# Batch 0 with more filler matmuls and a later exp, loads queued two batches ahead, attention moved within the experts' matmuls

## The chip, the cores and the metric

The kernel runs on one core of one Trainium2 chip. The metric is the device time of one execution in microseconds (us). Three runs of the kernel before gave 232.02, 232.46 and 232.63 us, median 232.46. The profile and the trace are of one further execution, which took 234.29 us. Engines are named as in the profile: PE (matrix multiplications; PEld is its weight load), ACT (activations), DVE (elementwise work), POOL (here it issues the loads), SP (here it issues the stores).

## What is computed

For each of 8 batches: linear attention over 8 heads (sequence 576, head size 64) with a normalisation, then one expert of 8 for the whole batch, chosen by a router on the mean over the sequence.

```python
kv  = einsum('bhsd,bhse->bhde', k, v)
out = einsum('bhsd,bhde->bhse', q, kv)
out = out / sqrt(mean(out * out, -1) + 1e-6) * g_norm
x   = out.transpose(0, 2, 1, 3).reshape(B, S, H * D)     # 8 x 576 x 512
logits = x.mean(1) @ w_gate                              # 8 experts
e_idx  = argmax(logits, 1)
y[b]   = softmax(logits)[b, e_idx] * (relu(x[b] @ w1[e_idx]) @ w2[e_idx])   # 512 -> 1024 -> 512
```

## The kernel before, in words

Everything is written for one batch at a time, and the order of the work on each engine is the order in which the program issues it. A load is converted from 32 to 16 bits on its way in.

The attention of a batch works on four pairs of heads, c = 0 to 3. Its pieces are small functions:

- `s_kv` (L115): 48 matmuls make k^T v of all pairs (12 for one pair), DVE casts them into the block matrices `kvb` (L128, L129). Called kv(b) here.
- `s_qt` (L102), called T(c): 12 transposes of q on PE, copied by DVE (L113).
- `s_o` (L131), called O(c): two matmuls (L135), then on ACT the square (L138), and on DVE a copy of the result (L143; batch 0 has none and reads PSUM later).
- `s_m` (L146), called M(c): two matmuls with `ones` take the mean of the squares (L151), then ACT does ln (L154) and exp (L155), which give one over the root.
- `s_x` (L158), called X(c): DVE multiplies and writes xT (L163), with the sum over the sequence as a by-product.
- `s_gate` (L167), `s_gate2` (L175), `s_gate3` (L203): the router. `s_gate2` has one small matmul (L178), finds the largest logit on DVE, POOL reads the index, and issues the loads of that expert's weights w1 (L194) and w2 (L196), called w(b), and behind them loads of q, k and v of a later batch (L64).

The expert of a batch (called MoE b) is cut into 18 units: 8 units `m_1` (L207; 8 matmuls L215 and a relu on ACT, L218) and 10 units `m_2` (L220; tiles t = 0 to 3 with 4 matmuls L244 a unit, and the smaller t = 4, L231). After two tiles DVE scales the result (L248, and L237 for t = 4) and SP stores it.

The program first runs the attention of batch 0 by itself, with filler matmuls (`warm`, L97; 128x512, into a tile that is written over) in between, then eight steps of batch 1. From there on it goes through the 8 x 18 units in order; after each unit it issues what the list `after` holds for that unit. `att_steps` (L284) cuts the attention of a batch into 17 steps, 0 to 16, for successive units: kv; T(0); T(1); O(0) and T(2); O(1); T(3) and M(0); O(2) and X(0); M(1); O(3) and X(1); M(2); M(3) and X(2); X(3) and gate; none; none; gate2; none; gate3. The line with `at` (L303) says behind which unit step 0 stands: unit 13 for batch 2, and unit 18(b-2)+3 for the others, so the attention of b runs within MoE b-2.

All loads that matter go through one queue, which POOL fills and which works in order. Four sets of q, k and v fit in SBUF, three sets of weights, and each PSUM tag ("a" for attention, "m" for the expert) has two buffers.

Of the kernel before, what the change touches and what calls it, by code (L numbers as in the profile page):

```python
# [17 lines left out]
def kernel(  # L18
# [36 lines left out]
    st = [dict() for _ in range(B)]  # L55

    def load_qkv(b, parts, which=None):
        if kvq[b] is None:
            kvq[b] = [pqkv.tile([P, H, NJ, Dh], F16, tag=n, name=n) for n in ("kt", "vt", "qt")]
        step = H // parts  # L60
        for i in (range(parts) if which is None else which):
            for t, src in zip(kvq[b], (k, v, q)):
                hs = slice(i * step, (i + 1) * step)
                nc.gpsimd.dma_start(  # L64
                    t[0:R, hs], src[b, hs].rearrange("h (p j) d -> p h (j d)", j=NJ))
# [25 lines left out]
    def psum(tag):  # L91
        return ps.tile([P, 2, 512], F32, tag=tag, name="ps_" + tag)

    def two(t):
        return t.rearrange("p (i n) -> p i n", i=2)

    def warm(t, n):  # L97
        for _ in range(n):
            nc.tensor.matmul(t[:, 1, :], ones, kvb[:, 1], start=True, stop=True)  # L99


    def s_qt(b, c, w=0):  # L102
        s = st[b]
        if "qT" not in s:
            s["qT"] = att.tile([P, NP, S], F16, tag="qT", name="qT")
        p32 = psum("a")
        warm(p32, w)
        pt = p32.bitcast(F16)
        for j in range(NJ):
            for i in range(2):  # L110
                nc.tensor.transpose(pt[64 * i:64 * i + 64, 0, j * R:(j + 1) * R],  # L111
                                    kvq[b][2][0:R, 2 * c + i, j, :], ident[0:R, 0:R])
        nc.vector.tensor_copy(s["qT"][:, c, :], pt[:, 0, 0:S])  # L113

    def s_kv(b, prs, w=0):  # L115
        kt, vt = kvq[b][0:2]
        kv = kvb[:, b % 2]
        p32 = psum("a")
        warm(p32, w)
        pk = p32[:, 0].rearrange("p (c e) -> p c e", c=NP)  # L120
        for c in prs:
            for j in range(NJ):
                for i in range(2):
                    nc.tensor.matmul(pk[64 * i:64 * i + 64, c, 64 * i:64 * i + 64],  # L124
                                     kt[0:R, 2 * c + i, j, :], vt[0:R, 2 * c + i, j, :],
                                     start=(j == 0), stop=(j == NJ - 1))
        cs = slice(prs[0], prs[-1] + 1)
        nc.vector.tensor_copy(kv[0:64, cs, 0:64], pk[0:64, cs, 0:64])  # L128
        nc.vector.tensor_copy(kv[64:128, cs, 64:128], pk[64:128, cs, 64:128])  # L129

    def s_o(b, c, tag="a"):  # L131
        s = st[b]
        po = psum(tag)
        for i in range(2):
            nc.tensor.matmul(po[:, i, 0:HS], kvb[:, b % 2, c, :],  # L135
                             s["qT"][:, c, i * HS:(i + 1) * HS], start=True, stop=True)
        sq = sm.tile([P, S], F16, tag="sq", name="sq")
        nc.scalar.activation(two(sq), po[:, :, 0:HS], AF.Square)  # L138
        if b == 0:
            o = po[:, :, 0:HS]  # L140
        else:
            o = two(sm.tile([P, S], F32, tag="o", name="o"))
            nc.vector.tensor_copy(o, po[:, :, 0:HS])  # L143
        s["sq", c], s["o", c] = sq, o

    def s_m(b, c):  # L146
        s = st[b]
        sq = s["sq", c]
        pm = psum("a")
        for i in range(2):  # L150
            nc.tensor.matmul(pm[:, i, 0:HS], ones, sq[:, i * HS:(i + 1) * HS],  # L151
                             start=True, stop=True)
        ln = sm.tile([P, S], F32, tag="ln", name="ln")
        nc.scalar.activation(two(ln), pm[:, :, 0:HS], AF.Ln, bias=epsc)  # L154
        nc.scalar.activation(ln, ln, AF.Exp, scale=-0.5)  # L155
        s["ln", c] = ln

    def s_x(b, c):  # L158
        s = st[b]
        if "xT" not in s:  # L160
            s["xT"] = xp.tile([P, NP, S], F16, tag="xT", name="xT")
            s["pl"] = sm.tile([P, NP], F32, tag="pl", name="pl")
        nc.vector.scalar_tensor_tensor(out=two(s["xT"][:, c, :]), in0=s["o", c], scalar=gcol,  # L163
                                       in1=two(s["ln", c]), op0=ALU.mult, op1=ALU.mult,
                                       accum_out=s["pl"][:, c:c + 1])
# [9 lines left out]
    def s_gate2(b):  # L175
        s = st[b]
        pg = psum("a")[:, 0, 0:E]
        nc.tensor.matmul(pg, mean, s["ts"], start=True, stop=True)  # L178
        mx = sm.tile([P, 8], F32, tag="mx", name="mx")
        ix = sm.tile([P, 8], U32, tag="ix", name="ix")  # L180
        nc.vector.max(mx, pg)
        nc.vector.max_index(ix, mx, pg)
        nm = sm.tile([P, 1], F32, tag="nm", name="nm")
        nc.vector.tensor_scalar(out=nm, in0=mx[:, 0:1], scalar1=-1.0, scalar2=None, op0=ALU.mult)
        lg = sm.tile([P, E], F32, tag="lg", name="lg")
        gs = sm.tile([P, 1], F32, tag="gs", name="gs")
        nc.scalar.activation(lg, pg, AF.Exp, bias=nm, accum_out=gs)
        ev = nc.gpsimd.value_load(ix[0:1, 0:1], min_val=0, max_val=E - 1)
        w1 = wp.tile([P, 4, F], F16, tag="w1", name="w1")
        w2 = wp.tile([P, 8, D], F16, tag="w2", name="w2")  # L190
        nh = 2 if b in (0, B - 1) else 1
        for h in range(nh):
            fs = slice(h * F // nh, (h + 1) * F // nh)
            nc.gpsimd.dma_start(w1[:, :, fs],  # L194
                                moe_w1[ds(ev, 1), :, fs].rearrange("o (c p) f -> p (o c) f", p=P))
        nc.gpsimd.dma_start(w2, moe_w2[ds(ev, 1)].rearrange("o (c p) d -> p (o c) d", p=P))  # L196
        s["w"] = (w1, w2)
        s["gs"] = gs
        for n in {0: (2,), 1: (3, 4)}.get(b, (b + 3,)):
            if n < B:  # L200
                load_qkv(n, 1)

# [62 lines left out]

    warm(psum("a"), 8)
    for c in range(NP):
        s_kv(0, [c], 1)  # L270
        s_qt(0, c, 1)
        if c > 0:
            s_m(0, c - 1)
        s_o(0, c, "m")
        if c > 0:
            s_x(0, c - 1)
    s_m(0, 3)
    warm(psum("a"), 9)
    s_x(0, 3)
    s_gate(0)  # L280
    s_gate2(0)


    def att_steps(b, early=False):  # L284
        T, M, X = (lambda c, f=f: (lambda: f(b, c)) for f in (s_qt, s_m, s_x))
        O = lambda c: (lambda: s_o(b, c, "m" if early and c < 3 else "a"))
        return [[lambda: s_kv(b, [0, 1, 2, 3], 4 if early else 0)],
                [T(0)], [T(1)], [O(0), T(2)], [O(1)], [T(3), M(0)], [O(2), X(0)], [M(1)],
                [O(3), X(1)], [M(2)], [M(3), X(2)], [X(3), lambda: s_gate(b)], [], [],
                [lambda: s_gate2(b)], [], [lambda: s_gate3(b)]]  # L290
# [7 lines left out]
    NU = 18  # L298
# [1 line left out]
    for i, e in enumerate(a1[n1:]):  # L300
        after[i] += e
    for b in range(2, B):
        at = 13 if b == 2 else NU * (b - 2) + 3  # L303
        for i, e in enumerate(att_steps(b)):
            after[at + i] += e
    for b in range(B):
# [34 lines left out]
```

## Time and profile before

| | |
|---|---|
| median of three runs | 232.46 us |
| the profiled execution, its own time | 234.29 us |
| its span in the trace | 232.6 us |
| PE busy | 193.7 us (83%) |
| ACT busy | 107.9 us (46%) |
| DVE busy | 98.0 us (42%) |
| POOL busy | 39.9 us (17%) |
| moved by DMA | 40.67 MB, mean 175 GB/s |

In the trace, the first unit of MoE 0 starts at 34.2 us, that of MoE 1 at 56.8, MoE 2 at 98.3, MoE 3 at 124.2, MoE 4 at 147.6, MoE 5 at 170.9, MoE 6 at 194.2 and MoE 7 at 210.5. A batch with attention in it takes 23.3 us from there on, one without 16.3 us.

How to read the lines: a row of waits gives the waiting engine with its line, who ended the wait, the sum in us, how often, and the longest. A row in order of time gives the start, the duration, the engine, the line, output<-input, shape and count; in square brackets stands how long the engine was idle before it and what released it. A row of stages gives, for a stretch of the span, the busy us and instructions of PE, PEld, DVE, ACT and POOL, then the clock granted to PE (1.00 is full), the busy share of the DMA engines and GB/s. A row of DMA issues ends with the KB and the us from issue to landing. The clock reads 1.00 until the first change that the record holds, so for the first stretch the durations have to tell it.

### The profile page before, as it was taken

How to read it: one execution, taken by the hardware profiler on the slowest of the kernel's cores; microseconds unless marked ns; L12 is line 12 of the kernel's file. 1: busy time of each engine (PE TensorE's matmuls, PEld its weight loads, DVE VectorE, ACT ScalarE, POOL GpSimd, SP SyncE). 2: the span in 40 equal slices, each digit the busy share in tenths (PEclk: the TensorE clock that was granted, in tenths of full speed). 3: DMA queues.
4: the chain of work that ended last, by engine and by line, in shares of the span. 5: the costliest groups of instructions: out<-in, count | busy, mean ns of one | idle time of the engine just before them, and what ended most of it. 6: DMA issues, size and time to landing. Idle time of an engine off the chain costs nothing.

```text
span 232.6 us, 4436 instructions
## 1 busy us (share of the span) xinstructions
PE 193.7 (83%) x1837; PEld 118.6 (51%) x1837; DVE 98.0 (42%) x232; ACT 107.9 (46%) x177; POOL 39.9 (17%) x58
## 2 busy tenths in 40 slices
PE   6896859997707989299898989898989898999990
PEld 1443436654505655167556755675567556747640
DVE  1243564246321449403394339533953385022040
ACT  2166079502903568034683468346834683504400
POOL 7920250280000006321002300200020002100000
PEclk9999999999965699859999999999999999999997
DMA  5999099999999905999999999999969933996033
GB/s 50 180 195 188 1 175 198 204 210 249 245 204 203 163 0 73 208 256 204 208 209 247 246 209 208 246 248 211 212 191 183 189 82 102 183 210 199 1 90 113
DMA packets 39141, 40.67 MB, mean 175 GB/s; under 512 B 2242, under 2 KB 31954, under 8 KB 39122
## 3 DMA queue, kind: packets, MB, share of 16 engines
q0 software_dynamic: 32592, 30.95, 83.4%
q1 hardware_dynamic: 6530, 9.44, 13.1%
q8 instruction: 14, 0.23, 0.4%
q14 instruction: 5, 0.04, 0.0%
HBM read 61.88 MB, written 9.44 MB: 307 GB/s over the span
## 4 chain that ended last, share of the span: by engine, by line
PE 46%; DMA 21%; ACT 12%; DVE 11%; issue 5%; POOL 1%; POOLq 1%; DVEq 0%
PE ps_m L215 25%; DMA vt<-in_v_dram 12%; PE ps_m L244 9%; DMA w<-in_moe_w_dram 7%; DVE ot L248 4%; ACT ln L154 4%; DVE o L143 3%; ACT sq L138 3%; PE ps_a L151 3%; PE ps_a L124 3%; DMA out_dram<-ot 3%; ACT hT L218 2%; PE ps_a L111 2%; PE ps_a L99 2%; DVE xT L163 2%
## 5 line engine op out<-in xcount | busy, mean ns | idle before, releaser
L215 PE MATMUL ps_m<-xT,w 128*128 128x288 f16 x512 | 73.9, 299 | 11.4 <-DMA w<-in_moe_w_dram 6.5
L218 ACT ACTIVATE hT<-ps_m 128x576 f16<-128x576 f32 x64 | 41.5, 650 | 52.9 <-PE ps_m L215 52.7
L215 PEld LDWEIGHTS <-w 128*128 128x128 f16 x512 | 50.5, 103 | 27.8 <-DMA w<-in_moe_w_dram 7.2
L244 PE MATMUL ps_m<-w,hT 128*128 128x512 f16 x256 | 61.8, 379 | 0.0
L244 PEld LDWEIGHTS <-hT 128*128 128x128 f16 x256 | 24.8, 98 | 22.8
L194 POOL DMA_DIRECT2D w<-in_moe_w_dram x10 | 7.6, 759 | 148.6 <-PE ps_m L215 58.6
L248 DVE TENSOR_SCALAR ot<-ps_m,gates 128x1024 f32<-128x1024 f32 x16 | 20.5, 1284 | 29.5 <-PE ps_m L244 27.3
L154 ACT ACTIVATE ln<-ps_a,epsc 128x576 f32<-128x576 f32 x32 | 23.6, 738 | 15.3 <-PE ps_a L151 15.2
L143 DVE COPY o<-ps_a 128x576 f32<-128x576 f32 x25 | 18.9, 756 | 27.5 <-ACT sq L138 27.5
L163 DVE SCALAR_TENSOR_TENSOR xT<-o,gcol,ln 128x576 f16<-128x576 f32 x28 | 22.4, 814 | 3.9 <-ACT ln L155 3.9
L155 ACT ACTIVATE ln<-ln 128x576 f32<-128x576 f32 x32 | 21.9, 683 | 1.0
L138 ACT ACTIVATE sq<-ps_a 128x576 f16<-128x576 f32 x25 | 16.0, 641 | 10.8 <-PE ps_a L135 10.2
L113 DVE COPY qT<-ps_a 128x576 f16<-128x576 f16 x32 | 14.5, 453 | 14.7 <-PE ps_a L111 14.6
L128 DVE CAST kvb<-ps_a 64x256 f16<-64x256 f32 (+1 forms) x11 | 3.8, 343 | 35.8 <-PE ps_a L124 35.8
L151 PE MATMUL ps_a<-sq,ones 128*128 128x288 f16 x64 | 14.6, 313 | 5.0 <-ACT sq L138 1.6
L111 PE MATMUL ps_a<-ident,qt 96*64 96x96 f16 x384 | 15.7, 223 | 2.2 <-ACT ln L154 0.9
L111 PEld LDWEIGHTS <-qt 96*64 96x64 f16 x384 | 11.3, 119 | 11.9 <-issue 9.3
L124 PE MATMUL ps_a<-vt,kt 96*64 96x64 f16 x384 | 9.3, 208 | 8.3 <-DMA vt<-in_v_dram 8.3
L99 PE MATMUL ps_a<-kvb,ones 128*128 128x512 f16 x29 | 13.2, 582 | 2.0 <-DVE ones L85 2.0
L124 PEld LDWEIGHTS <-kt 96*64 96x64 f16 x384 | 8.1, 123 | 13.1 <-issue 12.2
L151 PEld LDWEIGHTS <-ones 128*128 128x128 f16 x64 | 6.1, 102 | 11.2 <-issue 5.3
L135 PE MATMUL ps_a<-qT,kvb 128*128 128x288 f16 x50 | 10.2, 285 | 1.9 <-DVE o L143 1.8
(41 smaller groups left out, 103.1 us busy)
## 6 DMA issues: line engine op xcount, KB each, us to landing
w<-in_moe_w_dram POOLq DMA_DIRECT2D x14, 1024.0 KB, 16.3
out_dram<-ot SPq DMA_DIRECT2D x24, 192.0 KB, 5.1
kt<-in_k_dram POOLq DMA_DIRECT2D x7, 576.0 KB, 20.4
vt<-in_v_dram POOLq DMA_DIRECT2D x7, 576.0 KB, 22.5
qt<-in_q_dram POOLq DMA_DIRECT2D x7, 576.0 KB, 24.6
out_dram<-ot SPq DMA_DIRECT2D x40, 64.0 KB, 4.8
w<-in_moe_w_dram POOLq DMA_DIRECT2D x4, 512.0 KB, 7.2
out_dram<-ot SPq DMA_DIRECT2D x16, 128.0 KB, 5.1
```

Source lines behind the costliest of these rows:

```text
L111: nc.tensor.transpose(pt[64 * i:64 * i + 64, 0, j * R:(j + 1) * R], kvq[b][2][0:R, 2 * c + i, j, :], ident[0:R, 0:R])
L124: nc.tensor.matmul(pk[64 * i:64 * i + 64, c, 64 * i:64 * i + 64], kt[0:R, 2 * c + i, j, :], vt[0:R, 2 * c + i, j, :], start=(j == 0), stop ...
L138: nc.scalar.activation(two(sq), po[:, :, 0:HS], AF.Square)
L143: nc.vector.tensor_copy(o, po[:, :, 0:HS])
L151: nc.tensor.matmul(pm[:, i, 0:HS], ones, sq[:, i * HS:(i + 1) * HS], start=True, stop=True)
L154: nc.scalar.activation(two(ln), pm[:, :, 0:HS], AF.Ln, bias=epsc)
L155: nc.scalar.activation(ln, ln, AF.Exp, scale=-0.5)
L163: nc.vector.scalar_tensor_tensor(out=two(s["xT"][:, c, :]), in0=s["o", c], scalar=gcol, in1=two(s["ln", c]), op0=ALU.mult, op1=ALU.mult, a ...
L215: nc.tensor.matmul(ph[:, i, 0:HS], w1[:, c, fb * P:(fb + 1) * P], s["xT"][:, c, i * HS:(i + 1) * HS], start=(c == 0), stop=(c == 3))
L218: nc.scalar.activation(two(s["hT"][:, fb, :]), ph[:, :, 0:HS], AF.Relu)
L244: nc.tensor.matmul(po[:, t % 2, :], s["hT"][:, fc, t * P:(t + 1) * P], w2[:, fc, :], start=(fc == 0), stop=(fc == 7))
L248: nc.vector.tensor_scalar(out=ot, in0=po, scalar1=gates[:, b:b + 1], scalar2=None, op0=ALU.mult)
```

## The change

It has four edits. Batch 0 gets more fillers: 10 instead of 8 ahead of it, 2 instead of 1 in each call of `s_kv` and `s_qt`, and 3 ahead of the last M. In batch 0 the exp of a pair is issued behind the square of the next pair. The loads of q, k and v of batch b+2 are queued behind w(b) for all b; before, it was batch 2 behind w(0), batches 3 and 4 behind w(1) and b+3 behind w(b). And for batches 3 to 7, step 0 of the attention stands behind unit 18(b-2)+2b-2, which is 4, 6, 8, 10 and 12 units into MoE b-2 instead of 3 for all.

```diff
-    def s_m(b, c):
+    def s_m(b, c, exp=True):
...
         nc.scalar.activation(two(ln), pm[:, :, 0:HS], AF.Ln, bias=epsc)
+        s["ln", c] = ln
+        if exp:
+            s_e(b, c)
+
+    def s_e(b, c):
+        ln = st[b]["ln", c]
         nc.scalar.activation(ln, ln, AF.Exp, scale=-0.5)
-        s["ln", c] = ln
...
-        for n in {0: (2,), 1: (3, 4)}.get(b, (b + 3,)):
+        for n in (b + 2,):
             if n < B:
                 load_qkv(n, 1)
...
-    warm(psum("a"), 8)
+    warm(psum("a"), 10)
     for c in range(NP):
-        s_kv(0, [c], 1)
-        s_qt(0, c, 1)
+        s_kv(0, [c], 2)
+        s_qt(0, c, 2)
         if c > 0:
-            s_m(0, c - 1)
+            s_m(0, c - 1, False)
         s_o(0, c, "m")
         if c > 0:
+            s_e(0, c - 1)
             s_x(0, c - 1)
+    warm(psum("a"), 3)
     s_m(0, 3)
     warm(psum("a"), 9)
...
-        at = 13 if b == 2 else NU * (b - 2) + 3
+        at = 13 if b == 2 else NU * (b - 2) + 2 * b - 2
```

Three places show how rows move. The first is ACT's queue in batch 0, from the second row on (sq, ln: L138, L154; exp is L155 before and L161 after). Before:

```order
L138 ACTIVATE sq_170<-ps_m_167 128x576
L154 ACTIVATE ln_206<-ps_a_203,epsc_109 128x576
L155 ACTIVATE ln_206<-ln_206 128x576
L138 ACTIVATE sq_212<-ps_m_209 128x576
L154 ACTIVATE ln_251<-ps_a_248,epsc_109 128x576
L155 ACTIVATE ln_251<-ln_251 128x576
```

After:

```order
L138 ACTIVATE sq_174<-ps_m_171 128x576
L154 ACTIVATE ln_212<-ps_a_209,epsc_109 128x576
L138 ACTIVATE sq_217<-ps_m_214 128x576
L161 ACTIVATE ln_212<-ln_212 128x576
L154 ACTIVATE ln_259<-ps_a_256,epsc_109 128x576
L138 ACTIVATE sq_264<-ps_m_261 128x576
L161 ACTIVATE ln_259<-ln_259 128x576
```

The square of the next pair now stands between a pair's ln and its exp.

The second is POOL's queue from the weights of batch 1 to those of batch 2 (kt, vt, qt are k, v and q of one batch; w1 and w2 an expert's weights; ix the index that the router found). Before:

```order
L196 DMA w2_622<-in_moe_w2_dram 128x8x512
L64 DMA kt_625<-in_k_dram 96x8x384
L64 DMA vt_626<-in_v_dram 96x8x384
L64 DMA qt_627<-in_q_dram 96x8x384
L64 DMA kt_631<-in_k_dram 96x8x384
L64 DMA vt_632<-in_v_dram 96x8x384
L64 DMA qt_633<-in_q_dram 96x8x384
L188 TENSOR_LOAD ix_1106
L188 ISA x2
L194 ISA
L194 DMA w1_1123<-in_moe_w1_dram 128x4x1024
```

After:

```order
L201 DMA w2_636<-in_moe_w2_dram 128x8x512
L64 DMA kt_639<-in_k_dram 96x8x384
L64 DMA vt_640<-in_v_dram 96x8x384
L64 DMA qt_641<-in_q_dram 96x8x384
L193 TENSOR_LOAD ix_1094
L193 ISA x2
L199 ISA
L199 DMA w1_1111<-in_moe_w1_dram 128x4x1024
L201 ISA
L201 DMA w2_1112<-in_moe_w2_dram 128x8x512
L64 DMA kt_1115<-in_k_dram 96x8x384
L64 DMA vt_1116<-in_v_dram 96x8x384
```

Batch 3 (kt_625, now kt_639) keeps its place. Batch 4 (kt_631, now kt_1115) moves from ahead of batch 2's router and weights to behind them.

The third is DVE in the second half of MoE 2, where the attention of batch 4 runs (o is the copy L143, xT is X, ot the scaled output: L248 before, L253 after). Before:

```order
L113 COPY qT_1367<-ps_a_1459 128x576
L143 COPY o_1488<-ps_a_1483 128x576
L163 SCALAR_TENSOR_TENSOR xT_1490,pl_1491<-o_1421,gcol_85,ln_1476 128x576
L248 TENSOR_SCALAR ot_1507<-ps_m_1454,gates_119 128x1024
L143 COPY o_1518<-ps_a_1513 128x576
```

After:

```order
L143 COPY o_1473<-ps_a_1468 128x576
L253 TENSOR_SCALAR ot_1479<-ps_m_1420,gates_119 128x1024
L113 COPY qT_1405<-ps_a_1485 128x576
L143 COPY o_1515<-ps_a_1510 128x576
L168 SCALAR_TENSOR_TENSOR xT_1517,pl_1518<-o_1448,gcol_85,ln_1502 128x576
L143 COPY o_1539<-ps_a_1534 128x576
L168 SCALAR_TENSOR_TENSOR xT_1517,pl_1518<-o_1473,gcol_85,ln_1527 128x576
L253 TENSOR_SCALAR ot_1546<-ps_m_1505,gates_119 128x1024
L168 SCALAR_TENSOR_TENSOR xT_1517,pl_1518<-o_1515,gcol_85,ln_1555 128x576
```

The first scaling of an output now stands ahead of T(3) and of the first X, and the second one ahead of the last two X; before, all four X stood ahead of the second scaling. On PE, kv(3) moves behind one more unit of MoE 1 (unit 4, with M(2) of batch 2), and kv(4) from behind the fourth to behind the seventh unit of MoE 2.

## The prediction

> **What bounds the kernel now.** I read the page's busy shares and slices first, then PE's waits, then the time order around the longest waits.
>
> ```profile
> PE 193.7 (83%) x1837; PEld 118.6 (51%) x1837; DVE 98.0 (42%) x232; ACT 107.9 (46%) x177; POOL 39.9 (17%) x58
> PE   6896859997707989299898989898989898999990
> PEclk9999999999965699859999999999999999999997
> PE ps_a L124 <- DMA vt<-in_v_dram: 8.3, 2, 7.7
> PE ps_m L215 <- DMA w<-in_moe_w_dram: 6.5, 3, 4.2
> PE ps_m L215 <- DVE ot L248: 4.0, 5, 0.9
> ```
>
> PE is busy for 83% and no other engine reaches half, so PE's order and what PE waits for set the time. The PE row dips at the start, in slices 11 and 12 and in slice 16. The three rows of waits say what the dips are: one wait of 7.7 us for v, waits of up to 4.2 us for weights, and many small ones for an output tile. The clock row drops at the same two places.
>
> ```profile
> 70.16 1.49 PE L124 MATMUL ps_a<-vt,kt 96*64 96x64 f16 x48 [7.70 <-DMA vt<-in_v_dram]
> 79.50:80.00 0.50, 0.50 (x5) 0.36 (x4) 0.16 (x1) 0.31 (x1) 0.00 (x0) 0.77 1.21 207
> 85.51 0.28 PE L178 MATMUL ps_a<-ts,mean 128*128 128x8 f32 x2
> 88.58 9.69 DMA w<-in_moe_w_dram
> 98.32 6.67 PE L215 MATMUL ps_m<-xT,w 128*128 128x288 f16 x32 [4.18 <-DMA w<-in_moe_w_dram]
> 104.92 0.95 PE L124 MATMUL ps_a<-vt,kt 96*64 96x64 f16 x48
> 124.23 4.08 PE L215 MATMUL ps_m<-xT,w 128*128 128x288 f16 x32 [0.90 <-DVE ot L248]
> ```
>
> These rows are a chain. kv(3) starts at 70.16 when v of batch 3 lands; the router matmul of batch 2 follows at 85.51; its weights are issued at 88.58, and the first half takes 9.69 us; MoE 2 starts at 98.32; kv(4) at 104.92. The clock (the third figure from the end of a windows row) is back up at 79.7, where it averages 0.77. From 105 on PE hardly waits. A load that is issued late moves all that follows.
>
> **Prologue: a gain of 1.3 us, taken.** Batch 0 runs a ring over three engines.
>
> ```profile
> 2.04 4.02 PE L99 MATMUL ps_a<-kvb,ones 128*128 128x512 f16 x9 [2.04 <-DVE ones L85]
> 12.20 0.74 ACT L154 ACTIVATE ln<-ps_a,epsc 128x576 f32<-128x576 f32 x1 [1.99 <-PE ps_a L151]
> 13.57 0.63 ACT L138 ACTIVATE sq<-ps_m 128x576 f16<-128x576 f32 x1
> 15.04 0.64 PE L151 MATMUL ps_a<-sq,ones 128*128 128x288 f16 x2 [0.22 <-DVE kvb L129]
> 19.22 0.74 ACT L154 ACTIVATE ln<-ps_a,epsc 128x576 f32<-128x576 f32 x1 [1.51 <-PE ps_a L151]
> 21.94 0.74 ACT L154 ACTIVATE ln<-ps_a,epsc 128x576 f32<-128x576 f32 x1 [0.73 <-PE ps_a L151]
> 25.33 0.28 PE L178 MATMUL ps_a<-ts,mean 128*128 128x8 f32 x2
> 25.55 1.02 PE L99 MATMUL ps_a<-kvb,ones 128*128 128x512 f16 x4
> 84.40 0.41 PE L151 MATMUL ps_a<-sq,ones 128*128 128x288 f16 x2 [0.29 <-DVE o L143]
> ```
>
> The ring goes from one ln to the next in 3.51 us (two turns from 12.20 to 19.22): ln, exp, xT on DVE, the casts of the next kv, the mean matmul M. A filler takes 4.02/9 = 0.45 us here and 0.25 us at 25.55, so PE is at half speed up to there. The new start is 12 fillers, kv and 2 fillers without a gap, about 5.5 us. At 98.32 the rise took some 5.3 us of unbroken matmuls, so I expect full speed from about 7.5. Then transposes (0.69 to 0.45 for twelve, by the rows at 75.05 and 83.67 below), M (0.64 to 0.41) and kv with the fillers around it are quicker ahead of the first ln, which comes about 0.9 earlier. Against it: with exp behind the next square, the square's 0.63 is inside the ring, while M shrinks from 0.64 to 0.41. A turn costs 0.4 more, and there are two: 0.8 lost. At the end the last ln no longer waits behind that exp: 21.94 less 19.22 is 2.72, and becomes 2.1; 0.6 gained. The router matmul now ends the queue of nine fillers (25.33, when its input was ready at 24.7); at full speed those are over first: another 0.6. Sum -0.9 + 0.8 - 0.6 - 0.6 = -1.3. Bounds: -2.1 (no turn grows) and +2.3 (half speed throughout, below). The gain reaches the end, since w(0) and every load behind it queue on this router.
>
> A rule weighs against this step. The Trainium skill, page "TensorE: Matmul & The Clock Gate", section "Part 4: PE-mode transpose", says that transposes do not count as PE activity for the clock. By it the prologue, a fifth of it transposes, could stay at half speed and the term would be the +2.3 bound. The trace agrees only in part: at 83.67, with the clock up, twelve transposes take 0.45 us, against 0.69 at 75.05 with the clock down, so a raised clock holds through them; whether they help to raise it no row shows.
>
> **From kv(3) to w(2): -3.3 us.** vt(3) has the same loads ahead of it as before, so kv(3) keeps its 70.16 less the prologue. It now sits one unit later; PE does m_1 unit 4 and M(2) in the wait, which falls from 7.7 to about 6.1.
>
> ```profile
> 71.58 2.10 PE L215 MATMUL ps_m<-xT,w 128*128 128x288 f16 x8
> 73.47 0.69 PE L151 MATMUL ps_a<-sq,ones 128*128 128x288 f16 x2
> 75.05 0.69 PE L111 MATMUL ps_a<-ident,qt 96*64 96x96 f16 x12 [0.89 <-ACT ln L154]
> 83.67 0.45 PE L111 MATMUL ps_a<-ident,qt 96*64 96x96 f16 x12
> 84.65 1.02 PE L244 MATMUL ps_m<-w,hT 128*128 128x512 f16 x4
> ```
>
> Between kv(3) and the router of batch 2 (85.51 - 70.16 = 15.35) three pieces go: the unit, 1.89 (71.58 to 73.47), M(2) with the wait behind it, 1.58 (to 75.05), and T(3) with M(0), 0.98 (83.67 to 84.65), which come after the router now. That is 4.45, of which I give back 1.45, because about that much of what stays falls into the 9.5 us at half clock. Net -3.0, bounds -4.4 and -2. From router to issue took 3.07 (85.51 to 88.58), and 2.30 for batch 0 (25.33 to 27.63); I take -0.3 between 0 and -0.8.
>
> **A new wait at kv(4): +7.8 us.** This is the largest term.
>
> ```profile
> vt<-in_v_dram POOLq DMA_DIRECT2D x1, 576.0 KB, 22.3
> 90.99 0.78 POOL L64 DMA_DIRECT2D vt<-in_v_dram  x1
> 27.63 1.51 POOL L194 DMA_DIRECT2D w<-in_moe_w_dram  x2 [14.61 <-issue]
> 82.00:94.00 12.00, 11.08 (x79) 5.95 (x77) 8.79 (x23) 8.28 (x14) 3.95 (x5) 1.00 0.34 50
> ```
>
> Before, k/v/q of batch 4 went out before w(2), and the queue had run dry by 82, so kv(4) waited for nothing. Now they stand behind w(2), in the place of batch 5, whose v landed at 90.99 + 22.3 = 113.3, 24.7 us after w(2)'s issue. The 22.3 row is the larger of two; k comes 2.1 earlier. Nothing ahead of it in the queue is different, so I carry 24.7 over, give or take 1. Before, kv(4) came 104.92 - 88.58 = 16.3 after that issue; it is now 8.4 later. But three more m_1 units are done ahead of it (4.08/4 = 1.0 each, 3.2 with the change between forms): -3.2. As a check: w1(2) at 9.7, four units at half speed 6.6, the router 0.3, three units 3.2, so PE is there at 19.8 and waits 4.9. The DMA slots of 82 to 94 (share 0.34) lie idle even longer, which is the cause. A wait of 4.2 put the clock down at 98.32 and cost 6.67 - 4.08 = 2.6 over four units; the same again here: +2.6, between 0 (a wait under about 3) and 4.8 (half of the 9.5 us after 70.16). Sum 8.4 - 3.2 + 2.6 = +7.8. Later loads have 26 units of lead against 15 for batch 4, and PE is then the slower.
>
> **Attention placed 6 to 12 units into each MoE, instead of 3: +0.5 us.**
>
> ```profile
> 122.94 0.39 PE L178 MATMUL ps_a<-ts,mean 128*128 128x8 f32 x2 [0.26 <-DVE ts L172]
> 135.27 0.41 PE L135 MATMUL ps_a<-qT,kvb 128*128 128x288 f16 x2 [0.36 <-DVE o L143]
> 137.20 0.41 PE L151 MATMUL ps_a<-sq,ones 128*128 128x288 f16 x2 [0.29 <-DVE o L143]
> L248 DVE TENSOR_SCALAR ot<-ps_m,gates 128x1024 f32<-128x1024 f32 x16 | 20.5, 1284 | 29.5 <-PE ps_m L244 27.3
> 39.22 1.14 PE L215 MATMUL ps_m<-xT,w 128*128 128x288 f16 x8 [0.17 <-ACT hT L218]
> 41.10 2.12 PE L215 MATMUL ps_m<-xT,w 128*128 128x288 f16 x16 [0.74 <-ACT hT L218]
> ```
>
> A batch with attention has four waits now: 0.90 (124.23), 0.26, 0.36, 0.29, 1.81 in all, so 7.24 for batches 4 to 7. The first two go where X(3) falls behind the output copies; the other two stay, and the output copies of 1.28 in DVE's queue between square and copy of o lengthen them for batches 5 to 7: my count is 0.8, 1.05, 1.5, 1.5, sum 4.85. Nine m_1 units lose their 0.09 for a change of form: -0.8. Against it, ln and exp of late batches meet the relu of the next MoE. MoE 0 shows that with the steps of batch 1 (as batch 6 now): 0.17 + 0.74 = 0.9. Batch 7 has two more M there (each a ln of 0.74 and an exp of about that on ACT): 2.2; batch 5 one: 0.4. Sum 4.85 + 3.5 - 7.24 - 0.8 = +0.3, taken as +0.5, bounds -6.5 (no wait left but the relu's) and +4.
>
> **w(7): +0.7 us.**
>
> ```profile
> w<-in_moe_w_dram POOLq DMA_DIRECT2D x1, 512.0 KB, 5.6
> 202.02 7.07 PE L244 MATMUL ps_m<-w,hT 128*128 128x512 f16 x32
> 210.47 8.00 PE L215 MATMUL ps_m<-xT,w 128*128 128x288 f16 x64 [0.38 <-DVE ot L248]
> ```
>
> The router of batch 7 moves to unit 8 of MoE 6. Router to issue 2.1 to 2.3, first part 5.6: 7.8. From there PE has 7 units of 0.88, the last tile 1.06 and the 0.38: 7.6. I add 0.5 for output stores in the same engines; bounds 0 and 3.
>
> **Sum.** -1.3 - 3.3 + 7.8 + 0.5 + 0.7 = **+4.4 us**. The profiled execution took 234.29 us (span 232.6) and would become 238.7; it is 1.8 above the median of the runs, 232.46, and I predict against the median: **236.9 us**, slower by 1.9%.
>
> **Rivals.** (1) *Faster: the placement pays.* If ACT's bursts vanish behind the two ps_m buffers and no DVE wait grows, that term is -6.5 and the total -2.6: 229.9. It decides once four batches shorten by over 1.15 us each. For it: the 0.90 waits clearly come from DVE order. Against: 39.22 and 41.10 show relu waits reaching PE. Chance 0.12. (2) *No change: kv(4) waits under 3 us*, because w(2) goes out or lands 2 us sooner; then the clock stays up too: -2 - 2.6, total -0.2, 232.3. Against: 24.7 is a measured landing. Chance 0.10. (3) *The fillers do not raise the clock.* Sixteen more, at 0.43 each, of which the last groups hide: the router of batch 0 comes at 27.6 instead of 25.33: +2.3 for -1.3, 240.5. For it: nine fillers in a row, 4.02 us, did not raise it. Chance 0.14. The forecast has 0.64.
>
> Below 0.3% (0.7 us) a measurement of this kernel cannot tell a change from none. Faster 0.12, same 0.10, slower 0.78. The range leaves out rival 1 and about as little above rival 3: 232.2 to 241.2; without the rivals it would be 234.4 to 239.4.
>
> **What would show it.** Right: fillers of 0.22 us from about 7.5 on; ln to ln 3.9; batch 0's router near 24.0; a wait for v of about 6 us and a second, new one of 4 to 6 ending some 15 us after MoE 2's start, with the clock at 0.5 after it; relu waits at the start of MoE 6. Wrong: no second wait for v, or MoE 3 to 6 under 22.5 us each.

## The result and the profile after

Four runs of the changed kernel took 242.62 to 245.79 us, median 244.08; the kernel before, on the same chip, 232.55. The ratio is **1.050, interval 1.043 to 1.0575**: slower by 11.5 us, and above the range. Ratios and intervals here leave out the executions that were over 1.5% slower than the quickest of their kernel; the medians keep them, so a ratio is not always that of the medians. The profiled execution took 242.62 us (span 241.0), the quickest of its four, while the one of before was 1.8 us above its median; the two profiles therefore differ by 8.3 us only. The sums below are made between the profiles.

The page of the changed kernel: busy time, slices of PE, its clock and the DMA rate.

```profile
PE 191.5 (79%) x1850; PEld 116.6 (48%) x1850; DVE 98.2 (41%) x232; ACT 105.9 (44%) x177; POOL 39.9 (17%) x58
PE   6877778999259879149989988998889798986690
PEclk9999979999959999758999999999999999999798
GB/s 60 189 195 149 63 200 203 206 228 255 210 125 4 33 165 279 211 207 209 205 240 192 194 204 226 178 195 209 241 181 135 210 207 0 69 201 253 25 86 110
```

The rows of PE's waits in it (who was waited for, sum, times, longest):

```profile
PE ps_a L124 <- DMA vt<-in_v_dram: 15.5, 2, 8.5
PE ps_m L220 <- ACT hT L223: 4.2, 8, 0.8
PE ps_m L249 <- DMA w<-in_moe_w_dram: 3.8, 1, 3.8
PE ps_m L220 <- DMA w<-in_moe_w_dram: 3.6, 4, 1.5
```

PE fell from 83% to 79%. The wait for v now comes twice, 15.5 us against 8.3. Relu (hT) holds up the next unit eight times, 4.2 us in all (before twice, 0.9 us), and one group is new: L249, the second half of an expert, waits 3.8 us for weights. The slices, counted from one, show where: 17 and 18 (the second wait for v) and 37 and 38 (the last MoE), each with the clock down in it or beside it. The DMA engines stand nearly still in slices 13 and 14, as they did before in 15 and 16 (0 and 73 GB/s). (The prediction counts the slices from zero.)

The time order of PE in the changed kernel (start, duration, the wait in brackets); L220 and L249 are L215 and L244 of before.

```profile
68.97 1.49 PE L124 MATMUL ps_a<-vt,kt 96*64 96x64 f16 x48 [7.03 <-DMA vt<-in_v_dram]
78.79 0.28 PE L183 MATMUL ps_a<-ts,mean 128*128 128x8 f32 x2
105.51 1.49 PE L124 MATMUL ps_a<-vt,kt 96*64 96x64 f16 x48 [8.51 <-DMA vt<-in_v_dram]
123.33 1.91 PE L220 MATMUL ps_m<-xT,w 128*128 128x288 f16 x13 [0.96 <-DVE ot L253]
212.54 4.09 PE L220 MATMUL ps_m<-xT,w 128*128 128x288 f16 x32 [0.65 <-DMA w<-in_moe_w_dram]
217.17 4.09 PE L220 MATMUL ps_m<-xT,w 128*128 128x288 f16 x32 [0.53 <-DMA w<-in_moe_w_dram]
225.04 8.77 PE L249 MATMUL ps_m<-w,hT 128*128 128x512 f16 x32 [3.77 <-DMA w<-in_moe_w_dram]
```

Issues of weights from POOL's time order: first w(7) in the kernel before (its w(2), at 88.58, is among the prediction's rows), then w(2) and w(7) in the changed kernel:

```profile
196.28 1.49 POOL L194 DMA_DIRECT2D w<-in_moe_w_dram  x2 [21.68 <-DVE gates L204]
```

```profile
81.20 0.77 POOL L199 DMA_DIRECT2D w<-in_moe_w_dram  x1 [32.99 <-DVE qT L113]
206.61 1.49 POOL L199 DMA_DIRECT2D w<-in_moe_w_dram  x2 [24.54 <-DVE gates L209]
```

Before, w(7) went out 14.2 us ahead of the start of MoE 7 (210.47), now 5.9 us (212.54).

The start of the last scaling on DVE closes the account, first of before and then of the changed kernel:

```profile
226.62 0.47 DVE L237 TENSOR_SCALAR ot<-ps_m,gates 128x256 f32<-128x256 f32 x1
```

```profile
235.04 0.48 DVE L242 TENSOR_SCALAR ot<-ps_m,gates 128x256 f32<-128x256 f32 x1
```

| stretch | before, us | after, us | difference | the prediction's term |
|---|---|---|---|---|
| start to kv(3) | 70.16 | 68.97 | -1.2 | -1.3 |
| kv(3) to the issue of w(2) | 18.42 | 12.23 | -6.2 | -3.3 |
| issue of w(2) to kv(4) | 16.34 | 24.31 | +8.0 | +8.4 |
| kv(4) to MoE 3 | 19.31 | 17.82 | -1.5 | -0.6 (-3.2 + 2.6) |
| MoE 3 to MoE 7 | 86.24 | 89.21 | +3.0 | +0.5 |
| MoE 7 to the last scaling | 16.15 | 22.50 | **+6.3** | **+0.7** |
| sum | | | +8.4 | +4.4 |

The last row is the largest miss. The second row misses by 2.9 us the other way: from kv(3) to MoE 3 the profile is 0.3 us longer than before where the forecast had 4.5, so a part of the misses cancels in the sum. The +0.5 counts batches 4 to 7, of which batch 4 stands in the row above with -1.0 (0.8 for 1.81); put there, the forecast is -1.6 for that row and +1.5 for MoE 3 to MoE 7.

### The profile page after: what moved, and what is told of

The parts are those of the page before. It is cut to its first block, busy times and chain, and to the rows that moved or that the text cites. A ratio compares the mean times of both kernels' runs of the same rounds, so it can differ in the third digit from the quotient of the medians.

```text
span 241.0 us, 4459 instructions
## 1 busy us (share of the span) xinstructions
PE 191.5 (79%) x1850; PEld 116.6 (48%) x1850; DVE 98.2 (41%) x232; ACT 105.9 (44%) x177; POOL 39.9 (17%) x58
## 4 chain that ended last, share of the span: by engine, by line
PE 36%; DMA 31%; ACT 14%; DVE 9%; issue 5%; POOL 2%; POOLq 1%; SPq 0%; DVEq 0%
DMA vt<-in_v_dram 18%; PE ps_m L220 14%; PE ps_m L249 11%; DMA w<-in_moe_w_dram 10%; ACT ln L154 4%; ACT hT L223 4%; DVE ot L253 3%; ACT ln L161 3%; ACT sq L138 3%; DMA out_dram<-ot 3%; PE ps_a L99 3%; PE ps_a L124 3%; DVE o L143 3%; PE ps_a L111 2%; PE ps_a L135 1%
## 5 line engine op out<-in xcount | busy, mean ns | idle before, releaser
L220 PE MATMUL ps_m<-xT,w 128*128 128x288 f16 x512 | 72.3, 293 | 9.3 <-ACT hT L223 4.2
L249 PE MATMUL ps_m<-w,hT 128*128 128x512 f16 x256 | 63.7, 388 | 3.8 <-DMA w<-in_moe_w_dram 3.8
L220 PEld LDWEIGHTS <-w 128*128 128x128 f16 x512 | 50.5, 101 | 26.0 <-issue 8.0
L249 PEld LDWEIGHTS <-hT 128*128 128x128 f16 x256 | 24.0, 100 | 28.3 <-DMA w<-in_moe_w_dram 4.1
L138 ACT ACTIVATE sq<-ps_a 128x576 f16<-128x576 f32 x25 | 16.1, 643 | 39.9 <-PE ps_a L135 39.9
L253 DVE TENSOR_SCALAR ot<-ps_m,gates 128x1024 f32<-128x1024 f32 x16 | 20.5, 1281 | 32.0 <-PE ps_m L249 29.7
L143 DVE COPY o<-ps_a 128x576 f32<-128x576 f32 x25 | 18.9, 755 | 26.1 <-ACT sq L138 26.1
L154 ACT ACTIVATE ln<-ps_a,epsc 128x576 f32<-128x576 f32 x32 | 23.7, 739 | 13.3 <-PE ps_a L151 13.1
L161 ACT ACTIVATE ln<-ln 128x576 f32<-128x576 f32 x32 | 21.9, 683 | 0.9
L124 PE MATMUL ps_a<-vt,kt 96*64 96x64 f16 x384 | 9.3, 209 | 15.5 <-DMA vt<-in_v_dram 15.5
L151 PE MATMUL ps_a<-sq,ones 128*128 128x288 f16 x64 | 13.1, 285 | 6.3 <-DVE kvb L129 2.2
L111 PEld LDWEIGHTS <-qt 96*64 96x64 f16 x384 | 10.5, 111 | 12.1 <-issue 9.5
L111 PE MATMUL ps_a<-ident,qt 96*64 96x96 f16 x384 | 14.5, 212 | 2.2 <-DVE qT L113 0.9
L99 PE MATMUL ps_a<-kvb,ones 128*128 128x512 f16 x42 | 13.4, 452 | 2.0 <-DVE ones L85 2.0
L151 PEld LDWEIGHTS <-ones 128*128 128x128 f16 x64 | 5.8, 98 | 10.6 <-issue 5.9
```

Source lines behind the costliest of these rows:

```text
L220: nc.tensor.matmul(ph[:, i, 0:HS], w1[:, c, fb * P:(fb + 1) * P], s["xT"][:, c, i * HS:(i + 1) * HS], start=(c == 0), stop=(c == 3))
L249: nc.tensor.matmul(po[:, t % 2, :], s["hT"][:, fc, t * P:(t + 1) * P], w2[:, fc, :], start=(fc == 0), stop=(fc == 7))
L253: nc.vector.tensor_scalar(out=ot, in0=po, scalar1=gates[:, b:b + 1], scalar2=None, op0=ALU.mult)
```

## The experiments

Each ratio is to the kernel before on the same chip. Its median there was 232.2 to 232.3 us, and 233.5 for three of them: the new placement alone, the 42 fillers and the router ahead of kv(3).

**The prologue alone** (the kernel before with the edits of batch 0 and nothing else; the diff is from the changed kernel).

```diff
-        for n in (b + 2,):
+        for n in {0: (2,), 1: (3, 4)}.get(b, (b + 3,)):
...
-        at = 13 if b == 2 else NU * (b - 2) + 2 * b - 2
+        at = 13 if b == 2 else NU * (b - 2) + 3
```

> The kernel before with the edits of batch 0 alone (fillers, exp behind the next square). Theory: the router of batch 0 at 23.65 instead of 25.33, the loads and kv(3) 1.2 to 1.6 us earlier, nothing else different: 231.0 to 231.4 us. Rival (the gain is lost at the next wait for a load): 232.3 us.

231.12 us, ratio 1.001 (0.996 to 1.006). The profile shows the router of batch 0 at 23.45 us instead of 25.33, but the runs cannot tell a gain from none.

**The fillers alone, exp left behind its ln** (from the kernel before).

```diff
-    warm(psum("a"), 8)
+    warm(psum("a"), 10)
...
-        s_kv(0, [c], 1)
-        s_qt(0, c, 1)
+        s_kv(0, [c], 2)
+        s_qt(0, c, 2)
...
+    warm(psum("a"), 3)
     s_m(0, 3)
```

> The kernel before with the added fillers of batch 0 alone; exp stays right behind ln. Theory, the later exp costs a turn about 0.35 us twice and gives 0.6 back at the end: from ln to ln 3.3 us (3.51 before, 3.67 with the later exp), the last ln behind an exp, the router matmul of batch 0 at 23.3 to 23.7 us and 231 us in all, as with both edits. Rival, the later exp is what made the prologue shorter: the router at 24.3 or later and 231.7 or more.

231.61 us, ratio 0.999 (0.994 to 1.004), the router at 23.53. The ln of batch 0 in ACT's time order, with the fillers alone:

```profile
11.57 0.74 ACT L154 ACTIVATE ln<-ps_a,epsc 128x576 f32<-128x576 f32 x1 [1.35 <-PE ps_a L151]
14.84 0.74 ACT L154 ACTIVATE ln<-ps_a,epsc 128x576 f32<-128x576 f32 x1 [1.28 <-PE ps_a L151]
18.12 0.74 ACT L154 ACTIVATE ln<-ps_a,epsc 128x576 f32<-128x576 f32 x1 [1.28 <-PE ps_a L151]
20.61 0.74 ACT L154 ACTIVATE ln<-ps_a,epsc 128x576 f32<-128x576 f32 x1 [0.49 <-PE ps_a L151]
```

And in the changed kernel:

```profile
11.61 0.74 ACT L154 ACTIVATE ln<-ps_a,epsc 128x576 f32<-128x576 f32 x1 [1.35 <-PE ps_a L151]
15.28 0.74 ACT L154 ACTIVATE ln<-ps_a,epsc 128x576 f32<-128x576 f32 x1 [1.82 <-PE ps_a L151]
18.95 0.74 ACT L154 ACTIVATE ln<-ps_a,epsc 128x576 f32<-128x576 f32 x1 [1.82 <-PE ps_a L151]
20.72 0.74 ACT L154 ACTIVATE ln<-ps_a,epsc 128x576 f32<-128x576 f32 x1
```

A turn takes 3.27 us with the fillers and 3.67 with the later exp; the last step shrinks from 2.49 to 1.77. The later exp costs 0.4 twice and gives 0.7 back: nothing, as the prediction had it (+0.8 and -0.6).

**The old order of loads, all else as changed.**

```diff
-        for n in (b + 2,):
+        for n in {0: (2,), 1: (3, 4)}.get(b, (b + 3,)):
```

> The changed kernel with the old order of loads (batch 4 ahead of the weights of batch 2), fillers, exp and placement as changed. Theory (the new wait at kv(4) is real lost time): the 8.5 us wait for v ahead of kv(4) is gone, and with it the half clock behind it (4.2 us at half, 2.1 lost), so 10.6 us less than the changed kernel's 242.6: 232 us, and MoE 3 starts near 113 instead of 123.3. Rival (the load queue is the bound anyway): the time comes back as waits for the weights of batches 3 to 5, and the time stays above 238 us.

235.52 us, ratio 1.015 (1.0035 to 1.026), between what the two theories gave. Against the changed kernel's 1.050, the order of loads costs 3.5%, some 8 us. MoE 3 starts at 115.80 us, 7.5 earlier than in the changed kernel; PE's time order shows why not all of the expected 10.6 us come back: with k, v and q of batch 4 ahead of them again, w(2) and w(3) are late.

```profile
91.17 1.16 PE L220 MATMUL ps_m<-xT,w 128*128 128x288 f16 x8 [2.96 <-DMA w<-in_moe_w_dram]
115.80 1.52 PE L220 MATMUL ps_m<-xT,w 128*128 128x288 f16 x10 [2.50 <-DMA w<-in_moe_w_dram]
```

**The old placement, and the new placement alone.** The first is the changed kernel with

```diff
-        at = 13 if b == 2 else NU * (b - 2) + 2 * b - 2
+        at = 13 if b == 2 else NU * (b - 2) + 3
```

> The changed kernel with the old placement (step 0 three units into MoE b-2), fillers, exp and order of loads as changed. Theory (w(7) issued late costs 6.4 us in MoE 7, the late steps of batches 5 to 7 another 2.7 in MoE 3 to 6): both are gone, MoE 7 takes 16.3 us again and MoE 3 to 6 take 86.2; but kv(4) stands three units earlier and waits about 3 us longer for the same v, and kv(3) one unit earlier. 239 to 241 us. Rival (the loads alone carry the loss and the placement nothing): 244 us or more.

The second is the kernel before with that line the other way round.

> The kernel before with the new placement alone (old prologue, old order of loads). Theory, the placement by itself costs what MoE 3 to 7 show in the changed kernel: a wait of 3 to 4 us for the second part of w(7) with the clock down after it, MoE 3 to 6 together 2 to 3 us longer than 86.2, against 3 us gained where kv(3) moves one unit, most of which comes back as waits for w(2) and w(3): 235 to 237.5 us. Rival, the placement only costs together with the new order of the loads: within 1 us of the kernel before.

With the old placement 241.64 us, ratio 1.043 (1.028 to 1.057); with the new placement alone 236.93 us, ratio 1.021 (1.008 to 1.033). Placed the old way, MoE 3 to 5 are back at 23.3 us each, MoE 6 at 16.3, and MoE 7 has no wait for weights, which is worth 9.3 us (3.0 and 6.3 in the table); but MoE 3 only starts at 130.81 us instead of 123.33, with 9.1 us of wait for v at kv(4), and so little is left of it; the interval overlaps that of the changed kernel. Placed the new way, with the old loads, MoE 7 waits just as in the changed kernel:

```profile
219.25 8.62 PE L244 MATMUL ps_m<-w,hT 128*128 128x512 f16 x32 [3.94 <-DMA w<-in_moe_w_dram]
```

So the placement costs by itself, 2.1% or 4.8 us, and not by way of the loads. The rows show a gain and a loss in it: MoE 3 starts at 117.53 us (124.23 in the kernel before), but from there to the last scaling it takes 111.6 us instead of 102.4.

**Batch 7 at unit 8 instead of 12.**

```diff
-        at = 13 if b == 2 else NU * (b - 2) + 2 * b - 2
+        at = 13 if b == 2 else NU * (b - 2) + min(2 * b - 2, 8 if b == 7 else 99)
```

> The changed kernel with only batch 7 moved, from 12 to 8 units into MoE 5. Theory (w(7) is issued too late): its router comes four units, some 4.5 us, earlier, the weights land before MoE 7 asks for them, the waits of 0.65, 0.53 and 3.77 us and the half clock after them (1.7 us) go, 6.5 us less than the changed kernel: 236 to 238 us. Rival (the stores of MoE 6 and 5 slow the load down wherever it stands): a wait of 2 us or more for the weights stays, 240 us or more.

237.33 us, ratio 1.026 (1.015 to 1.038). One batch carries about half of the whole loss. From MoE 7 to the last scaling it takes 17.4 us instead of 22.5, and MoE 3 to 6 are 1.0 us shorter. w(7) goes out at 201.07 us, 9.5 ahead of MoE 7, and of the last wait for it 1.04 us is left, with the clock up behind it (7.08 us for what took 8.77):

```profile
219.58 7.08 PE L249 MATMUL ps_m<-w,hT 128*128 128x512 f16 x32 [1.04 <-DMA w<-in_moe_w_dram]
```

**No stores for batch 6** (its output is never written): is w(7) only late, or do the stores of MoE 6, which run in the same DMA engines, hold it up?

```diff
-                for i in range(2):
+                for i in range(2 if b != 6 else 0):
                     nc.sync.dma_start(ob[NJ - 1, R - 64:R, i * D // 2:(i + 1) * D // 2],
...
-            for i in range(2):
+            for i in range(2 if b != 6 else 0):
                 col = (t - 1 + i) * P
```

> The changed kernel without the ten stores of batch 6 (its output stays unwritten). Theory, the stores share the DMA engines with w(7): from the issue of w(7) to the end of its second part 18.4 us passed in the changed kernel (206.61 to 225.04), in which w1, w2 and the stores moved about 3.3 MB; without the stores' 1.2 MB the same rate brings w2 in some 12 us after the issue, before PE asks for it. The wait of 3.77 us goes, the clock stays up, MoE 7 to the last scaling takes 17 to 18 us instead of 22.6, and the whole is 5 us shorter than the changed kernel. Rival, w(7) is only issued too late: the wait for the second part stays over 2.5 us and under 2 us are gained.

238.82 us, ratio 1.0265 (1.014 to 1.039): 5 us of the 11.5 gone. In the time order (POOL, then PE), w(7) goes out even later than in the changed kernel and the wait is all but gone; from MoE 7 to the last scaling it takes 17.1 us.

```profile
208.54 1.49 POOL L199 DMA_DIRECT2D w<-in_moe_w_dram  x2 [24.89 <-DVE gates L209]
222.98 7.36 PE L249 MATMUL ps_m<-w,hT 128*128 128x512 f16 x32 [0.29 <-DMA w<-in_moe_w_dram]
```

From the issue to the start of L249 it is 14.4 us against 18.4. The windows of the changed kernel say how full the engines were in those 18.4 us (last figures of a row: clock, DMA share, GB/s).

```profile
208.00:212.00 4.00, 3.90 (x30) 1.91 (x28) 1.83 (x2) 0.00 (x0) 1.00 (x2) 1.00 0.97 141
212.00:218.00 6.00, 4.92 (x39) 3.73 (x40) 0.62 (x2) 2.60 (x4) 0.00 (x0) 1.00 1.13 229
218.00:222.00 4.00, 3.27 (x27) 2.36 (x25) 0.00 (x0) 2.60 (x4) 0.00 (x0) 1.00 1.18 256
222.00:225.00 3.00, 0.00 (x0) 0.00 (x0) 0.00 (x0) 0.00 (x0) 0.00 (x0) 1.00 0.67 111
```

That is 3.3 MB in 17 us (4 x 141 + 6 x 229 + 4 x 256 + 3 x 111 KB): 2.1 MB of w(7), the rest output. Both hold: the issue is late by its place, and the stores make the late issue hurt.

**Fillers in the wait at kv(4)**, 32 and then 42 (the diff of the first; the second has 42 in place of 32).

```diff
-        return [[lambda: s_kv(b, [0, 1, 2, 3], 4 if early else 0)],
+        return [[lambda: s_kv(b, [0, 1, 2, 3], 4 if early else 32 if b == 4 else 0)],
```

> The changed kernel with 32 filler matmuls (about 7 us) ahead of kv(4), inside its wait of 8.5 us. Theory, the fall of the clock behind that wait has a price of its own: kv(4) still starts 24.3 us after the issue of w(2), with a wait of 1 to 1.5 us left; from kv(4) to the start of MoE 3 15.7 us instead of 17.8; the whole about 2 us shorter than the changed kernel. Rival, the 2 us at half speed are swallowed by later waits: MoE 3 starts as before, under 0.5 us gained.

> The changed kernel with 42 filler matmuls ahead of kv(4), where 32 left a wait of 1.92 us and the clock fell all the same. At 0.22 us each they end about when v of batch 4 lands, 23 to 24.3 us after the issue of w(2). Theory, the fall of the clock behind the wait costs some 2 us: the wait at kv(4) is under 0.7 us, the clock stays up, and from kv(4) to the start of MoE 3 it is 15.5 to 16.2 us instead of 17.8 (17.5 with 32 fillers). Rival, the stretch is as long as before for other reasons, such as waits for DVE: 17 us or more.

With 32 fillers 241.59 us, ratio 1.045 (1.034 to 1.056); with 42, 241.74 us, ratio 1.038 (1.023 to 1.053). Both intervals overlap that of the changed kernel, so the total decides nothing; the rows do. With 32:

```profile
95.26 7.07 PE L99 MATMUL ps_a<-kvb,ones 128*128 128x512 f16 x32
104.24 0.95 PE L124 MATMUL ps_a<-vt,kt 96*64 96x64 f16 x48 [1.92 <-DMA vt<-in_v_dram]
105.13 2.10 PE L220 MATMUL ps_m<-xT,w 128*128 128x288 f16 x8
```

With 42:

```profile
98.53 9.23 PE L99 MATMUL ps_a<-kvb,ones 128*128 128x512 f16 x42
107.69 0.95 PE L124 MATMUL ps_a<-vt,kt 96*64 96x64 f16 x48
108.57 1.15 PE L220 MATMUL ps_m<-xT,w 128*128 128x288 f16 x8
```

The first of the two expectations failed: the 1.92 us that were left put the clock down all the same (2.10 us for eight matmuls against 1.15), and from kv(4) to MoE 3 it was still 17.5 us. Without a gap it was 16.5 us (107.69 to 124.18), a wait of 0.42 for q of batch 4 among it; that lies between the theory (15.5 to 16.2) and its rival (17 or more). The clock's share of the wait at kv(4) is 1.3 us (17.8 less 16.5), or 1.8 without that small wait; the prediction had 2.6.

**k of batch 2 loaded ahead of w(0)** (with the prologue's edits and the old loads and placement; the last argument of `load_qkv` picks among k, v and q).

```diff
     load_qkv(1, 1)
+    load_qkv(2, 1, None, (0,))
...
-                load_qkv(n, 1)
+                load_qkv(n, 1, None, (1, 2) if n == 2 else (0, 1, 2))
```

> The kernel before with the prologue of the changed one, and k of batch 2 loaded right behind batch 1 instead of behind the weights of batch 0. Theory, the wait for v of batch 3 (7.9 us) comes from a queue that is full from w(0) on but nearly idle from 22.9 to 25.8 us (12 GB/s): k of batch 2 fits in there, all later transfers land 2 to 3 us earlier, the wait for v at kv(3) is 5 to 6 us, and the whole 2 to 3 us shorter than the 231.1 with the prologue alone. Rival, w(0) then lands later by what k of batch 2 takes and MoE 0 starts later: 231 or more.

232.25 us, ratio 0.998 (0.993 to 1.003). The gap was filled: the window 22.90 to 25.80 us moved 184 GB/s instead of 12. But kv(3) came only 1.4 us earlier (68.31 with the prologue alone), and its wait did not shrink:

```profile
66.95 1.49 PE L125 MATMUL ps_a<-vt,kt 96*64 96x64 f16 x48 [7.91 <-DMA vt<-in_v_dram]
```

PE had come earlier by as much. The theory falls, and the total is the rival's, though MoE 0 did not start later (31.34 us; 31.69 with the prologue alone). Where the rest of the 2 to 3 us went was not followed further.

**The router of batch 2 ahead of kv(3).** The changed kernel, its loads included, with another placement.

```diff
-        at = 13 if b == 2 else NU * (b - 2) + 2 * b - 2
+        at = 13 if b == 2 else NU * (b - 2) + {3: 9, 4: 9, 5: 8, 6: 7, 7: 6}[b]
```

> The changed kernel with its order of loads, but with the attention of batches 3 to 7 placed 9, 9, 8, 7 and 6 units into the MoE, so that the router of batch 2 stands ahead of kv(3) on PE. Theory, the order of loads loses only because w(2) goes out late, behind PE's wait for v of batch 3, and so batch 4 lands later still: with the router ahead of that wait w(2) is issued at about 69 us instead of 81.2, directly behind the loads of batch 3; kv(3) waits under 3 us, kv(4) under 4, MoE 3 starts at 107 to 112 us instead of 123.3, w(7) goes out early enough, and the whole takes 217 to 224 us, less than both kernels. Rival, the queue is then full throughout and the waits move to the weights of MoE 3 to 6: 228 us or more.

**224.27 us, ratio 0.964 (0.947 to 0.981)**: faster than both kernels, and some 20 us faster than the changed one, by one line. The median is 0.3 above the expected 217 to 224. The line moves batches 3, 4, 6 and 7, so the rows, and not the total, have to say which part is the router's. The slices of its page, PE and clock:

```profile
PE   6977639899898899859889997988998989999980
PEclk9999985999999999999999999999999999999997
```

Its waits:

```profile
PE ps_a L111 <- DMA qt<-in_q_dram: 3.4, 4, 1.0
PE ps_m L220 <- ACT hT L223: 3.3, 7, 0.7
PE ps_a L124 <- DMA vt<-in_v_dram: 2.1, 2, 1.6
```

And the rows of its time order (PE and POOL) that answer to those of the changed kernel:

```profile
71.05 0.28 PE L183 MATMUL ps_a<-ts,mean 128*128 128x8 f32 x2
71.26 0.95 PE L124 MATMUL ps_a<-vt,kt 96*64 96x64 f16 x48
73.09 0.77 POOL L199 DMA_DIRECT2D w<-in_moe_w_dram  x1 [22.76 <-issue]
97.16 0.95 PE L124 MATMUL ps_a<-vt,kt 96*64 96x64 f16 x48 [1.65 <-DMA vt<-in_v_dram]
```

kv(3) no longer waits, since PE does the rest of batch 2 while v of batch 3 lands; w(2) goes out 8.1 us earlier than in the changed kernel (12 were expected; MoE 0 and MoE 1 began late in this execution), behind the loads of batch 3; and v of batch 4, still behind w(2), is there 24.1 us later, when PE has little else to wait for. MoE 3 starts at 110.00 us instead of 123.33; that kv(4) stands three units later has a part in this that no run separates. After the first 40 us the clock stays up. No weights are waited for in MoE 2 to 7; the rival, that the waits move to them, did not come about.

**The same with the old order of loads.**

```diff
-        for n in (b + 2,):
+        for n in {0: (2,), 1: (3, 4)}.get(b, (b + 3,)):
```

> The kernel with the router of batch 2 ahead of kv(3), but with the old order of loads. Theory, the new order of loads has a value of its own once w(2) goes out early: with k, v and q of batch 4 (some 9 us of transfers) still ahead of w(2) in the queue, MoE 2 starts 5 to 7 us later than the 83.9 us of the kernel with the new loads, later weights are waited for too, and the whole is 3 to 8 us longer than its 224.3. Rival, the gain is the placement's alone and the order of loads does not matter there: within 1.5 us of it.

224.27 us, ratio 0.972 (0.959 to 0.985). The equal medians favour the rival, but four runs of each, on two chips, leave a difference of some 2% either way open: 8 us are out, 3 are not. The first half of the theory was seen. PE waits for w(2) and loses its clock:

```profile
86.89 2.10 PE L220 MATMUL ps_m<-xT,w 128*128 128x288 f16 x8 [6.34 <-DMA w<-in_moe_w_dram]
```

But MoE 3 starts at 111.62 us, 1.6 later than with the new loads, and MoE 7 at 199.40, 0.8 earlier: the waits for k, v and q of later batches are gone, since those are loaded ahead. Of the two orders one pays at w(2) and the other in small waits later. These starts do not favour the new order: its execution was 2.6 us behind at MoE 0 already (33.35 against 30.76), where the two programs are still the same, and 2.7 at MoE 1. From the start of MoE 1 to the last scaling it took 158.7 us, the old order 160.7. So the new order may be worth some 2 us here, in one execution of each. Most of the gain of 8 us over the kernel before comes with the placement under either order, as the prologue alone gave nothing that the runs can tell.

## Why the prediction was wrong

- **w(7), +0.7 predicted, +6.3 measured: the step that failed.** The term followed the load only to its first part (issue 2.1 to 2.3 us after the router, 5.6 us to land) and set that against PE's 7.6 us. That part was right: PE waited 0.65 us at 212.54. But behind it in the queue come the second half of w1 and then w2, which PE needs 4.1 and 8.7 us after the start of MoE 7. They were 0.53 and 3.77 us late, and the last wait put the clock down (8.77 - 7.08 = 1.7 us): 6.0 us together. The stores, priced at 0.5, belong to this: without them the 3.77 us are 0.29. The upper bound of 3 stands without a working of its own and is half of what came. With 6.3 in the place of 0.7 alone the forecast is 242.5 us, above its range.
- **The placement, +1.5 predicted for MoE 3 to 6 (+0.5 with batch 4), +3.0 measured.** The waits were sized rightly, the busy time was not. The windows of MoE 3 to 6, before and after (us, busy time of PE first), and the wait for relu in the second:

```profile
124.23:210.47 86.24, 80.41 (x791) 51.27 (x790) 40.31 (x93) 45.85 (x76) 9.61 (x12) 1.00 1.04 199
```

```profile
123.33:212.54 89.21, 81.23 (x792) 50.89 (x792) 42.97 (x99) 44.69 (x77) 11.92 (x15) 1.00 0.97 175
PE ps_m L220 <- ACT hT L223: 3.2, 6, 0.8
```

  PE's idle time grew from 5.8 to 8.0 us. The relu has 3.2 us of it (3.5 were counted), the waits for DVE 3.7 (4.05 counted for these three batches), and w(7) adds 0.27 at the end. PE's busy time grew by 0.8 where I had taken 0.8 off for fewer changes of form: the steps that leave the m_1 units of one MoE come to stand between the halves of its last tile (4.3 to 4.8 us) and, for batches 5 to 7, between the m_1 units of the next (m_1 in all 34.1 to 34.7 us). Rival 1, that the placement pays, is refuted by the new placement alone, which is 2.1% slower; with the new loads the totals of the two placements cannot be told apart.
- **The new wait at kv(4): right.** The landing 24.7 us after the issue of w(2), carried over from batch 5, came at 24.3. The wait was 8.5 us instead of 4.9 because PE got there sooner: MoE 2 started at 89.83, 1.48 us late instead of 4.18, and its first units ran at full clock. Such a wait only absorbs what PE gained, so the sum was unharmed. Undoing the loads gave back 8 us, net of new waits for w(2) and w(3); the term was +7.8, and that the two agree so closely is in part luck. Rival 2 (a wait under 3 us) is out. Its premise, that a short wait leaves the clock up, fell with the 32 fillers.
- **kv(3) to w(2): -6.2 instead of -3.3.** 4.45 us of work moves out of this stretch; I gave 1.45 back for half clock. The clock came up 3.3 us after kv(3) instead of 9.5, so nothing was given back, and there was more to gain.
- **The prologue: -1.2 against -1.3 in the profiles.** That the two agree to 0.1 us is luck. The parts had the right signs but other sizes: the first ln -0.6 (-0.9 predicted), the turns +0.3 (+0.8), the last step -0.95 (-0.6), the way to the router -0.5 (-0.6), -1.7 in all at the router; and in the six profiled kernels whose PE has the same work up to kv(3), it starts anywhere from 67.68 to 70.17 us. In the runs the gain is not to be told from nothing. Rival 3 is refuted: twelve transposes took 0.45 us from 8.16 us on, 0.69 before. (Its sixteen more fillers are thirteen: L99 has 29 matmuls on the page of before and 42 after.) The rule of the Trainium skill that was weighed there (page "TensorE: Matmul & The Clock Gate", section "Part 4: PE-mode transpose") did not show here: with transposes about a fifth of PE's busy time (1.78 of 9.93 us from 7.27 to 20.50), the prologue kept the raised clock.

One thing the prediction did not see at all: kv(3) stands ahead of the router of batch 2, and so v of batch 3 delays w(2), whatever the loads' order. It named the chain, took it as given, and priced the new order of loads on it. With the router first, the runs cannot tell the two orders of loads apart: the 8 us that the new order loses hang on that chain. Of what this placement gains over the changed kernel, 13.3 us lie ahead of MoE 3 and 6.4 behind the start of MoE 7 (22.50 less 16.14 us to the last scaling), since w(7) goes out early; in between it loses 0.9.

## What to carry to other kernels

Where a load is chosen by the result of earlier work, put that work ahead of any wait for another load on the same engine. Follow a late issue to its last byte, against the moment when each part is needed, with all other traffic of that stretch in the sum; the first part says little. And an order of loads cannot be judged apart from the order in which the engine asks for them: the same two orders were 3.5% apart under one placement and, within what the runs can tell, level under another.

## What was unexpected of the hardware

The length of a wait did not decide whether the clock fell. It was down after waits of 0.94 us (MoE 0, without the stores; gaps of 0.80 and 0.58 us stand shortly ahead of it), 1.92 us (32 fillers), 2.84 us (MoE 2, placement alone), 3.14 us (MoE 7, 42 fillers) and, 1.2 us late, 2.50 us (MoE 3, old loads), and stayed up after 1.56 us (MoE 2, without the stores), 2.96 us (MoE 2, old loads) and 3.04 us (MoE 7, 32 fillers). Nor is the time to come back fixed: after kv(3) 3.3 us in the changed kernel, 9.5 in the one before. The Trainium skill (page "TensorE: Matmul & The Clock Gate", section "Part 1: The HAM clock gate (the "warmup" mystery)") has the clock follow the activity in windows of about 3.4 us that run freely. By it a wait shorter than such a window should leave the clock up; five of the eight here did not, nor do the 9.5 us follow from it, and what decides stays open. It may be part of why single runs of one kernel spread so far, but no run here shows that: the kernel before took from 229.95 to 235.06 us in nineteen runs, the prologue alone 229.47 to 234.45 in ten.
